# Attention and SwiGLU on one core: matrix products grouped by array shape, weights converted 1536 columns at a time with paced loads, gains on another queue

## The chip, the cores and the metric

The kernel runs on one core of a Trainium2 chip. The metric is the device time of one execution in microseconds (us), as the median of several runs. Engines are called TensorE (PE in the profile, PEld for its weight loads), VectorE (DVE), ScalarE (ACT), GpSimd (POOL) and SyncE (SP, which here only issues transfers).

## The reference, cut to what matters

```python
# q, k, v: (8, 12, 448, 64); d_model 768, d_ff 1536; the weights come as float64
q_n, k_n = rmsnorm(q, g_q), rmsnorm(k, g_k)
attn = softmax(q_n @ k_n.T / 8)
x = (attn @ v) -> (3584, 768)
g = x @ w_gate
out = (g * sigmoid(g) * (x @ w_val)) @ w_out
```

## The kernel before

Two heads are a "pair"; a batch has 6 pairs, and there are 48. The MLP works on 7 blocks of 512 tokens. Block n needs the attention of batches n and n+1. So batches 0 and 1 (12 "early" pairs) come first, together with the conversion of the float64 weights to float32, done by bit operations on ScalarE and VectorE. After that, the attention of batch n+2 is fitted in beside block n.

The program itself writes the order of the instructions. Every piece of work (one or some instructions of one engine) is registered with an estimated duration, a wished time `when`, and what it depends on. A small list scheduler at build time then simulates the engines and emits the pieces in the order that it finds:

```python
def start(self, piece):
    at = self.free.get(piece["engine"], 0.0)
    ...
    for before in piece["after"]:
        if before["end"] is None:
            return None
        at = max(at, before["end"] + 0.1)
    ...  # and the users of the buffers that it takes
# run(): for each engine, the first piece in order of `when`, unless another
# can start more than 0.02 us sooner
```

For one pair, scores `S_j = K_j^T Q` for four quarters j use 64 rows of the array for each head (row tiling). The weighted sums use 64 columns for each head (column tiling), with four quarters accumulated in PSUM (the memory that TensorE writes its sums to), and a fifth product with ones for the denominator. (Early pairs do the denominator in all four quarters.) The MLP and the transposes use the full array:

```python
when = base + (j // 2) * span * 0.4 + (j % 2) * 0.1          # score j
... 
last = add("PE", 1.55 if early else 0.8,                     # weighted sum j
           base + span * (0.55 + (j // 2) * 0.25) + (j % 2) * 0.1,
           lambda j=j: weighted(j), after=[ex[j], load_v, last], ...)
```

A part of the weights (768 columns) is loaded to a staging place inside tiles that are not in use yet, then takes six instructions:

```python
loaded = add("SP", 0.45, when - 14.0, lambda: nc.sync.dma_start(raw, src), after=[before], kb=768)
one   = add("ACT", 0.91, when, ... activation(dst, hi, AF.Abs) ...)
two   = add("ACT", 0.91, when, ... activation(lo, lo, AF.Copy, scale=2.0**-29) ...)
three = add("DVE", 0.56, when, ... tensor_scalar_max(dst, dst, LEAST) ...)
four  = add("DVE", 0.57, when, ... tensor_scalar(shift left 3, and) ...)
five  = add("DVE", 0.97, when, ... scalar_tensor_tensor(and, or) ...)
six   = add("DVE", 0.97, when, ... tensor_tensor(add) ...)
```

## Time and profile before

| | before |
|---|---|
| time, median | 1863.93 us (1863.9 to 1864.73) |
| first up projection of block 0 | 200.29 us |
| changes of array shape on TensorE before / after that point | 75 / 479 |
| from there to the end of the last matmul | 1657.8 us |
| TensorE, VectorE busy between 20 and 150 us | 110.2 / 107.4 of 130 us |
| mean granted TensorE clock between 20 and 150 us | 0.92 |

Read it as two programs one after the other. Up to 200 us, waits among all engines set the time; from then on TensorE is never idle for more than 0.6 us at a time. The lines are shown in the prediction. A change of array shape is counted where two neighbouring TensorE pieces use different tilings (full, 64 rows, 64 columns).

### The profile page before, as it was taken

What the parts mean: (1) busy time and instruction counts of PE and PEld (TensorE: products, weight loads), DVE (VectorE), ACT (ScalarE), POOL (GpSimd) and SP (SyncE); (2) the same over time, 40 slices, a digit from 0 to 9 for tenths busy, and PEclk for the clock granted to TensorE, in tenths of its full rate; (3) what the DMA queues carried; (4) which work ended last, traced back from release to release, by engine and by line L of the source; (5) the groups of instructions that cost most, each with busy time, mean ns of one, the idle gap of its engine ahead of it and who ended that gap; (6) DMA issues with size and microseconds to landing.
All of it is one profiled execution on the core that took longest, in us unless ns stands there. A gap on an engine that the chain in (4) does not pass through costs nothing.

```text
span 1863.5 us, 13867 instructions
## 1 busy us (share of the span) xinstructions
PE 1806.0 (97%) x5616; PEld 780.7 (42%) x5616; DVE 497.3 (27%) x568; ACT 387.6 (21%) x556; POOL 507.2 (27%) x264
## 2 busy tenths in 40 slices
PE   5788999999999999999999999999999999999998
PEld 2322344444444443444434444444444333444455
DVE  5887711132211231112231122221123121101100
ACT  6865310122101220102211022110122111100000
POOL 3784420254100542104432025320155122200000
PEclk9899999999999999999999999999999999999999
DMA  9645200011000110001110011100011000000000
GB/s 284 198 138 166 75 10 0 18 58 33 5 10 14 43 34 24 10 2 36 46 31 10 0 33 43 39 10 0 14 43 45 13 5 11 13 18 5 0 9 27
DMA packets 55053, 73.35 MB, mean 39 GB/s; under 512 B 4804, under 2 KB 44228, under 8 KB 54980
## 3 DMA queue, kind: packets, MB, share of 16 engines
q1 hardware_dynamic: 45888, 61.35, 11.1%
q10 hardware_dynamic: 8964, 11.02, 2.0%
q8 instruction: 46, 0.75, 0.2%
q14 instruction: 27, 0.22, 0.0%
q0 software_dynamic: 128, 0.00, 0.0%
HBM read 61.34 MB, written 11.01 MB: 39 GB/s over the span
## 4 chain that ended last, share of the span: by engine, by line
PE 92%; issue 3%; POOL 2%; ACT 1%; DVE 1%; ACTq 0%; POOLq 0%
PE mm L872 47%; PE mm L932 24%; PE at L705 11%; PE st L658 8%; PE st L620 2%; POOL rr L588 1%; POOL t L600 1%; ACT e L668 1%; DVE inv L744 0%; DVE QT L641 0%; ACT KT L633 0%; DVE wo L852 0%; DVE wo L845 0%; ACT wo L820 0%; ACT wo L824 0%
## 5 line engine op out<-in xcount | busy, mean ns | idle before, releaser
L932 PE MATMUL mm<-wo,gt 128*128 128x384 f32 x1344 | 458.4, 493 | 0.6 <-ACT rows L942 0.6
L872 PE MATMUL mm<-xT,wv 128*128 128x512 f32 x1008 | 450.7, 596 | 0.6 <-ACT rows L942 0.6
L872 PE MATMUL mm<-xT,wg 128*128 128x512 f32 x1008 | 450.3, 596 | 0.0
L932 PEld LDWEIGHTS mm<-wo,gt 128*128 128x128 f32 x1344 | 248.0, 190 | 218.4 <-issue 61.1
L872 PEld LDWEIGHTS mm<-xT,wv 128*128 128x128 f32 x1008 | 188.0, 190 | 249.8 <-issue 248.6
L674 POOL TENSOR_TENSOR sums<-e 112x896 f32<-112x896 f32 x36 | 75.2, 2089 | 790.2 <-ACT e L668 790.2
L872 PEld LDWEIGHTS mm<-xT,wg 128*128 128x128 f32 x1008 | 187.8, 190 | 244.1 <-issue 222.4
L668 ACT ACTIVATE e<-st 112x896 f32<-112x896 f32 x192 | 172.1, 916 | 333.2 <-PE st L658 251.3
L588 POOL TENSOR_TENSOR rr<-ss,minus_half 112x16 f32<-112x16 f32 x48 | 169.9, 3541 | 203.8 <-DVE ss L580 202.3
L744 DVE RECIPROCAL inv<-at 128x448 f32<-128x448 f32 x48 | 141.8, 2955 | 236.1 <-PE at L705 236.1
L658 PE MATMUL st<-QT,KT 64*112 64x448 f32 x768 | 190.7, 594 | 11.5 <-DVE QT L641 6.4
L882 ACT ACTIVATE gt<-mm 128x512 f32<-128x512 f32 x84 | 50.2, 597 | 689.4 <-PE mm L872 689.4
L705 PE MATMUL at<-e,v 112*64 112x448 f32 x768 | 188.7, 570 | 3.0 <-DVE inv L744 2.9
L677 POOL TENSOR_TENSOR sums<-sums,e 112x896 f32<-112x896 f32 x72 | 149.5, 2076 | 128.2 <-ACT e L668 126.1
L885 DVE SCALAR_TENSOR_TENSOR gt<-gt,mm 128x512 f32<-128x512 f32 x84 | 57.7, 687 | 435.9 <-ACT gt L882 435.9
L890 DVE SCALAR_TENSOR_TENSOR gt<-gt,mm 128x512 f32<-128x512 f32 x84 | 57.7, 687 | 338.9 <-PE mm L872 338.9
L658 PEld LDWEIGHTS st<-QT,KT 64*112 64x112 f32 x768 | 57.5, 177 | 136.2 <-issue 88.0
L600 POOL TENSOR_TENSOR t<-qk,rr 112x512 f32<-112x512 f32 x96 | 110.5, 1170 | 3.2
L641 DVE TENSOR_SCALAR QT<-st,gg 128x448 f32<-128x448 f32 x42 | 28.5, 678 | 254.9 <-ACT KT L633 254.5
L942 ACT COPY rows<-mm 128x384 f32<-128x384 f32 x56 | 26.8, 478 | 312.5 <-PE mm L932 312.5
L705 PEld LDWEIGHTS at<-e,v 112*64 112x64 f32 x768 | 39.7, 136 | 112.8 <-issue 102.0
L620 PE MATMUL st<-ident,t 112*128 112x112 f32 x384 | 50.0, 273 | 34.8 <-POOL t L600 31.9
(55 smaller groups left out, 525.2 us busy)
## 6 DMA issues: line engine op xcount, KB each, us to landing
qk<-in_q_dram SPq DMA_DIRECT2D x48, 224.0 KB, 2.8
qk<-in_k_dram SPq DMA_DIRECT2D x48, 224.0 KB, 2.9
v<-in_v_dram SPq DMA_DIRECT2D x48, 224.0 KB, 2.8
wo<-in_moe_w_out_dram SPq DMA_DIRECT2D x8, 768.0 KB, 4.3
gt<-in_moe_w_gate_dram SPq DMA_DIRECT2D x6, 768.0 KB, 12.0
gt<-in_moe_w_val_dram SPq DMA_DIRECT2D x6, 768.0 KB, 14.3
wo<-in_moe_w_gate_dram SPq DMA_DIRECT2D x6, 768.0 KB, 12.8
wo<-in_moe_w_val_dram SPq DMA_DIRECT2D x6, 768.0 KB, 11.5
```

The source lines that it names most:

```text
L588: nc.gpsimd.tensor_tensor(out=rr.rearrange("p x h j one -> p (x h j one)"), in0=tiles["ss", m], in1=minus_half, op=ALU.pow,)
L600: nc.gpsimd.tensor_tensor(out=tiles["t", m][:, :, x].rearrange("p j h d -> p h j d"), in0=tiles["qk", (m, x)], in1=tiles["rr", m][:, x].to ...
L620: nc.tensor.transpose(ps[:, x, ts(j, R)], tiles["t", m][:, j, x].rearrange("p h d -> p (h d)"), ident[0:R, 0:R],)
L658: nc.tensor.matmul(st[0:R, h, 0:S], tiles["KT", m][rows, j, :], tiles["QT", m][rows].rearrange("p j r -> p (j r)"), start=True, stop=True,)
L668: nc.scalar.activation(e, tiles["st", (m, j)][0:R, :, 0:S], AF.Exp)
L674: nc.gpsimd.tensor_tensor(out=to, in0=tiles["e", (m, 0)], in1=e, op=ALU.add)
L677: nc.gpsimd.tensor_tensor(out=to, in0=to, in1=e, op=ALU.add)
L705: nc.tensor.matmul(to[ds(D * h, D), 0:S], lhs(h), rhs[:, h], start=first, stop=last)
L744: nc.vector.reciprocal(inv, tiles[den][:, 0:S])
L872: nc.tensor.matmul(ps, w[:, f // 2, c, ts(f % 2, P)], xT[:, c, ts(n % 2, TB)], start=(c == 0), stop=(c == NW - 1),)
L885: nc.vector.scalar_tensor_tensor(gt[:, f], gt[:, f], 1.0, tiles["mm", (n, f, 0)], op0=ALU.add, op1=ALU.mult)
L932: nc.tensor.matmul(ps[:, 0:HALF], gt[:, f, ts(i, P)], wo[:, f, ts(half, HALF)], start=(f == 0), stop=(f == NF - 1),)
```

## The change

Its intent: change the array shape less often; give the first pairs of the attention priority over the conversion of the weights; and save instructions. Its core (cuts marked by `...`):

```diff
-            at = max(at, before["end"] + 0.1)
+            at = max(at, before["end"] + 0.1 * (before["engine"] != piece["engine"]))
...
+        if piece["early"] is not None:
+            at = max(at, piece["when"] - piece["early"])
...  # run(): a piece of the group just issued goes next if it can start within 0.7 us
+                    if last["group"] and piece["group"] == last["group"] and at < self.free[engine] + 0.7:
+                        choice = (at, piece)
+                        break
...  # scores: two and two, one right after the other
-            when = base + (j // 2) * span * 0.4 + (j % 2) * 0.1
+            when = base + (j // 2) * 0.4 + (j % 2) * 0.01
+                group=("s", m, j // 2), mode="rows",
...  # weighted sums and denominator: one group, after the first scores of the next pair
+        late = c == NPAIR - 1 and not early
+        when = base + span * 0.8 if late else sum(pair_time(m + 1)[:1]) + 0.2
+                after=(ex if j == 0 else []) + [load_v, last], group=("w", m), mode="columns",
...  # weights: 18 parts of 1536 columns
-        when = 8.0 + 5.0 * n
+        when = 12.0 + 11.0 * n
-            "SP", 0.45, when - 14.0, ..., after=[before], kb=768
+            "SP", 0.45, when - 16.0, ..., after=[staged.get(place)], kb=1536, early=2.0,
...  # queries of all early pairs on ScalarE (before: of every second one)
-            if early and m % 2:
+            if early:
...  # gains
-        nc.gpsimd.dma_start(t[0:64, :], col)
+        nc.scalar.dma_start(t[0:64, :], col)
-    nc.vector.scalar_tensor_tensor(out=gg, in0=gq2, scalar=8.0, in1=gk2, ...)
+    scaled_gains = order.add("DVE", 0.2, 9.0, lambda: nc.vector.scalar_tensor_tensor(out=gg, ...), early=0.0)
```

The loads of q, k and v also got `early=25.0`, and up projections wait in the model for the end of the block before.

More of the change, by code (lines that the diff above doesn't have):

```diff
@@ L361 @@
 class Order:
+    SWITCH = 0.17
     def __init__(self, pools):
@@ L378, in __init__, with add @@
         self.dma = 0.0
-    def add(self, engine, us, when, emit, after=(), takes=(), uses=(), port=False, kb=0):
+        self.last = {}
+    def add(
+        self, engine, us, when, emit, after=(), takes=(), uses=(), port=False, kb=0, group=None,
+        mode=None, early=None,
+    ):
         piece = dict(
             engine=engine, us=us, when=when, emit=emit, takes=takes, port=port, kb=kb,
+            group=group, mode=mode, early=early,
             after=[a for a in after if a is not None], end=None, n=len(self.pieces),
@@ L414, in run @@
                 choice = None
+                last = self.last.get(engine, dict(group=None))
                 for piece in pieces[:lookahead]:
                     at = self.start(piece)
-                    if at is not None and (choice is None or at < choice[0] - 0.02):
+                    if at is None:
+                        continue
+                    if (
+                        last["group"]
+                        and piece["group"] == last["group"]
+                        and at < self.free[engine] + 0.7
+                    ):
+                        choice = (at, piece)
+                        break
+                    if choice is None or at < choice[0] - 0.02:
                         choice = (at, piece)
@@ L427, in run @@
             end = at + piece["us"]
+            last = self.last.get(piece["engine"])
+            if piece["mode"] and last and last["mode"] != piece["mode"]:
+                end += self.SWITCH
+            self.last[piece["engine"]] = piece
             self.free[piece["engine"]] = end
@@ L513, in fast @@
     FIRST = LEAD + EARLY * PAIR + 10.0
-    UP, DOWN, BOTH = 122.0, 63.0, 113.0
+    UP, DOWN, BOTH = 123.6, 63.0, 113.0
     def block_start(n):
@@ L548, in load @@
             when = base - (26.0 if name == "qk" else 16.0)
-            return add("SP", 0.45, when, emit, takes=[(name, key)], kb=224)
+            return add("SP", 0.45, when, emit, takes=[(name, key)], kb=224, early=25.0)
         loaded = [load("qk", (m, x), src) for x, src in enumerate((q, k))]
@@ L626, in attention @@
         transposed = add(
-            "PE", 0.95, base - 3.0, transpose, after=scaled, uses=[("t", m)],
-            takes=[("st", (m, "t"))],
+            "PE", 0.8, base - 3.0, transpose, after=scaled, uses=[("t", m)],
+            takes=[("st", (m, "t"))], mode="full",
         )
@@ L647, in attention @@
         qt = add(
-            "ACT" if early and m % 2 else "DVE", 0.68, base - 1.5, queries, after=[transposed],
+            "ACT" if early else "DVE", 0.68, base - 1.5, queries, after=[transposed],
             takes=[("QT", m)], uses=[("st", (m, "t"))],
@@ L680, in attention @@
         for j in range(NJ):
-            when = base + (j // 2) * span * 0.4 + (j % 2) * 0.1
+            when = base + (j // 2) * 0.4 + (j % 2) * 0.01
             st = add(
-                "PE", 0.82, when, lambda j=j: scores(j), after=[kt, qt],
+                "PE", 0.75, when, lambda j=j: scores(j), after=[kt, qt],
                 uses=[("KT", m), ("QT", m)], takes=[("st", (m, j))],
+                group=("s", m, j // 2), mode="rows",
             )
@@ L723, in attention @@
             last = add(
-                "PE", 1.55 if early else 0.8,
-                base + span * (0.55 + (j // 2) * 0.25) + (j % 2) * 0.1,
-                lambda j=j: weighted(j), after=[ex[j], load_v, last],
+                "PE", 1.5 if early else 0.75, when + j * 0.01, lambda j=j: weighted(j),
+                after=(ex if j == 0 else []) + [load_v, last],
                 takes=([av, den] if early else [av]) if j == 0 else [],
                 uses=[("e", (m, j)), ("v", m)] + ([av] + [den] * early if j else []),
+                group=("w", m), mode="columns",
             )
@@ L737, in attention @@
             last = add(
-                "PE", 0.9, base + span * 0.95, total, after=[last, adds[-1]],
-                uses=[("sums", m)], takes=[den],
+                "PE", 0.75, when + 0.05, total, after=[last, adds[-1]],
+                uses=[("sums", m)], takes=[den], group=("w", m), mode="columns",
             )
@@ L746, in attention @@
         inv = add(
-            "DVE", 2.96, base + span, invert, after=[last], uses=[den], takes=[("inv", m)]
+            "DVE", 2.96, when + 4.0, invert, after=[last], uses=[den], takes=[("inv", m)]
         )
@@ L766, in attention @@
         done_x[m] = add(
-            "DVE", 0.66, base + span + 1.0, divide, after=[inv] + [up_done[n] for n in blocks],
+            "DVE", 0.66, when + 5.0, divide, after=[inv] + [up_done[n] for n in blocks],
             uses=[av, ("inv", m)],
@@ L781, in weight_parts, with weight_part @@
         gate, val = (w.rearrange("(c p) f -> p c f", p=P) for w in (moe_w_gate, moe_w_val))
+        places = [("gt", 0), ("gt", 1), ("wo", 0), ("wo", 1), ("wo", 2)]
         n = 0
         for f in range(NF // 2):
-            for half in range(2):
-                for w, dst, name in ((gate, wg, "g"), (val, wv, "v")):
-                    cs = ts(half, NW // 2)
-                    where = n % 10
-                    stage = ("gt", where) if where < 4 else ("wo", where - 4)
-                    yield w[:, cs, ts(f, 2 * P)], dst[:, f, cs, :], (NW // 2, 2 * P), (name, f), stage
-                    n += 1
+            for w, dst, name in ((gate, wg, "g"), (val, wv, "v")):
+                yield w[:, :, ts(f, 2 * P)], dst[:, f], (NW, 2 * P), (name, f), places[n % 5]
+                n += 1
         rows = moe_w_out.rearrange("(f p) c -> p f c", p=P)
-        for f in range(NF):
-            stage = ("wo", (5, 4, 3)[f % 3]) if f < 8 else ("gt", 2 + f % 2)
-            yield rows[:, f : f + 1, :], wo[:, f : f + 1, :], (1, DM), ("o", f), stage
+        for f, place in enumerate((4, 3, 4, 4, 1, 1)):
+            fs = ts(f, 2)
+            yield rows[:, fs, :], wo[:, fs, :], (2, DM), ("o", f), places[place]
     weights = {}
     staged = {}
-    def weight_part(n, src, dst, shape, what, stage):
-        a, b = shape
-        before = staged.get(stage)
-        when = 8.0 + 5.0 * n
-        region, s = stage
+    def weight_part(n, src, dst, shape, what, place):
+        when = 12.0 + 11.0 * n
+        region, s = place
         if region == "gt":
-            raw = gt[:, ts(s, NF // 4), :].rearrange("p f t -> p (f t)")
+            raw = gt[:, ts(s, NF // 2), :].rearrange("p f t -> p (f t)")
         else:
-            raw = wo[:, ts(s, 2), :].rearrange("p f c -> p (f c)")
-        raw = raw.bitcast(I64).rearrange("p (a b) -> p a b", a=a)
+            raw = wo[:, ts(s, NF // 3), :].rearrange("p f c -> p (f c)")
+        raw = raw.bitcast(I64).rearrange("p (a b) -> p a b", a=shape[0])
         words = raw.bitcast(U32).rearrange("p a (b two) -> p a b two", two=2)
@@ L815, in weight_part @@
         loaded = add(
-            "SP", 0.45, when - 14.0, lambda: nc.sync.dma_start(raw, src), after=[before], kb=768
+            "SP", 0.45, when - 16.0, lambda: nc.sync.dma_start(raw, src),
+            after=[staged.get(place)], kb=1536, early=2.0,
         )
@@ L819, in weight_part @@
         one = add(
-            "ACT", 0.91, when, lambda: nc.scalar.activation(dst, hi.bitcast(F32), AF.Abs),
+            "ACT", 1.55, when, lambda: nc.scalar.activation(dst, hi.bitcast(F32), AF.Abs),
             after=[loaded, *clear],
@@ L823, in weight_part @@
         two = add(
-            "ACT", 0.91, when, lambda: nc.scalar.activation(lo, lo, AF.Copy, scale=2.0**-29),
+            "ACT", 1.55, when, lambda: nc.scalar.activation(lo, lo, AF.Copy, scale=2.0**-29),
             after=[loaded],
@@ L827, in weight_part @@
         three = add(
-            "DVE", 0.56, when, lambda: nc.vector.tensor_scalar_max(dst, dst, LEAST),
+            "DVE", 0.95, when, lambda: nc.vector.tensor_scalar_max(dst, dst, LEAST),
             after=[one], port=True,
@@ L831, in weight_part @@
         four = add(
-            "DVE", 0.57, when,
+            "DVE", 0.97, when,
             lambda: nc.vector.tensor_scalar(
@@ L843, in weight_part @@
         five = add(
-            "DVE", 0.97, when,
+            "DVE", 1.77, when,
             lambda: nc.vector.scalar_tensor_tensor(
@@ L850, in weight_part @@
         six = add(
-            "DVE", 0.97, when,
+            "DVE", 1.77, when,
             lambda: nc.vector.tensor_tensor(out=bits, in0=bits, in1=lo, op=ALU.add),
@@ L854, in weight_part @@
         )
-        staged[stage] = six
-        weights.setdefault(what, []).append(six)
+        staged[place] = weights[what] = six
     down_done = {}
@@ L894, in block @@
         hidden = []
-        last = None
+        last = down_done.get(n - 1)
         for f in range(NF):
@@ L900, in block @@
                     add(
-                        "PE", 5.05, start + (2 * f + which) * step,
+                        "PE", 5.15, start + (2 * f + which) * step,
                         lambda f=f, which=which: gate_value(f, which),
                         after=[done_x[m] for m in tokens]
-                        + (weights["gv"[which], f // 2] if n == 0 else []) + [last],
-                        takes=[("mm", (n, f, which))],
+                        + ([weights["gv"[which], f // 2]] if n == 0 else []) + [last],
+                        takes=[("mm", (n, f, which))], mode="full",
                     )
@@ L909, in block @@
             when = start + 2 * f * step + 1.0
-            before = [down_done[n - 1]] if n else [staged.get(("gt", f // 3))]
+            before = [down_done[n - 1]] if n else [staged.get(("gt", f // (NF // 2)))]
             t = add(
@@ L964, in block @@
                     + (
-                        [w for f in range(part * NF // 2, (part + 1) * NF // 2) for w in weights["o", f]]
+                        [weights["o", f // 2] for f in range(part * NF // 2, (part + 1) * NF // 2)]
                         if n == 0 else []
                     ),
-                    takes=[key] * (1 - part), uses=[key] * part,
+                    takes=[key] * (1 - part), uses=[key] * part, mode="full",
                 )
@@ L986, in fast @@
         col = x.rearrange("(d one) -> d one", one=1)
-        nc.gpsimd.dma_start(t[0:64, :], col)
-        nc.gpsimd.dma_start(t[64:128, :], col)
+        nc.scalar.dma_start(t[0:64, :], col)
+        nc.scalar.dma_start(t[64:128, :], col)
     make_identity(nc, ident)
     nc.gpsimd.memset(ones, 1.0)
-    nc.vector.scalar_tensor_tensor(
-        out=gg, in0=gq2, scalar=8.0, in1=gk2, op0=ALU.mult, op1=ALU.mult
+    scaled_gains = order.add(
+        "DVE", 0.2, 9.0,
+        lambda: nc.vector.scalar_tensor_tensor(
+            out=gg, in0=gq2, scalar=8.0, in1=gk2, op0=ALU.mult, op1=ALU.mult
+        ),
+        early=0.0,
     )
```

## The prediction

> **What bounds the kernel now.** I read the page's slices first, then the chain of waits, then the timeline of TensorE.
>
> ```profile
> PE 1806.0 (97%) x5616; PEld 780.7 (42%) x5616; DVE 497.3 (27%) x568; ACT 387.6 (21%) x556; POOL 507.2 (27%) x264
> ...
> PE   5788999999999999999999999999999999999998
> ...
> DVE  5887711132211231112231122221123121101100
> PEclk9899999999999999999999999999999999999999
> ...
> PE 92%; issue 3%; POOL 2%; ACT 1%; DVE 1%; ACTq 0%; POOLq 0%
> ```
>
> A slice is 46.6 us. The first four or five hold the attention of two batches and the conversion of the weights (12 early pairs of heads); there TensorE has holes and VectorE is at 7 to 8 tenths. From then on TensorE is full, so every microsecond of TensorE work saved there is saved in the end. The windows of the early stretch (columns: length, busy of PE, PEld, DVE, ACT, POOL, clock, DMA share, GB/s):
>
> ```profile
> 0.00:10.00 10.00, 0.00 (x0) 0.00 (x0) 0.56 (x3) 2.74 (x4) 3.19 (x12) 1.00 0.58 168
> 10.00:20.00 10.00, 0.00 (x0) 0.00 (x0) 6.08 (x10) 4.61 (x6) 4.67 (x2) 1.00 1.08 285
> ...
> 40.00:60.00 20.00, 13.00 (x58) 5.33 (x56) 18.65 (x24) 15.08 (x21) 8.31 (x4) 0.75 0.92 267
> 60.00:80.00 20.00, 17.17 (x74) 5.90 (x72) 16.05 (x21) 17.39 (x23) 17.48 (x6) 0.82 0.63 192
> ```
>
> TensorE does nothing for 20 us, then loses 7 us of the 20 after 40 us, while the queues move 267 to 380 GB/s of weights. The first cause is on VectorE and GpSimd:
>
> ```profile
> 13.66 0.16 DVE L991 SCALAR_TENSOR_TENSOR gg<-gq,gk 128x1 f32<-128x1 f32 x1 [9.53 <-DMA gk<-in_g_k_dram]
> 13.74 1.21 DVE L579 TENSOR_REDUCE ss<-t 112x16 f32<-112x1024 f32 x1
> ...
> 20.84 2.01 PE L620 MATMUL st<-ident,t 112*128 112x112 f32 x8 [20.84 <-POOL t L600]
> ```
>
> ScalarE had squared the first q and k by 5.56 us, but VectorE stood behind the product of the two gains, whose DMA landed only at 13.6. Now a stretch of the full phase; the third view shows what a change of array shape costs:
>
> ```profile
> 262.62 5.42 PE L872 MATMUL mm<-xT,wg 128*128 128x512 f32 x12
> 267.97 1.01 PE L658 MATMUL st<-QT,KT 64*112 64x448 f32 x4
> 268.91 5.42 PE L872 MATMUL mm<-xT,wv 128*128 128x512 f32 x12
> 274.17 5.31 PE L872 MATMUL mm<-xT,wg 128*128 128x512 f32 x12
> 279.31 5.31 PE L872 MATMUL mm<-xT,wv 128*128 128x512 f32 x12
> ...
> 339.93 0.97 PE L705 MATMUL at<-e,v 112*64 112x448 f32 x4
> 340.83 4.14 PE L932 MATMUL mm<-wo,gt 128*128 128x384 f32 x12
> 344.90 0.97 PE L705 MATMUL at<-e,v 112*64 112x448 f32 x4
> ```
>
> From start to start (the durations overlap), twelve up-projection instructions take 5.15 us when the next has the same shape (274.17 to 279.31) and 5.35 before a score (262.62 to 267.97). A score takes 0.94 before a full-array matmul, but 0.75 when another score follows (eight in 1.69). A weighted sum takes 0.90 before a down projection and 0.75 before another weighted sum. So each change costs 0.15 to 0.20 us.
>
> **What the Trainium skill says.** (1) "TensorEngine Tiling (Array Packing)", section "Key Properties": "Changing tiling mode (not just tile) drains the TensorE". The trace agrees: the 0.15 to 0.20 us above appear at changes between 64-row, 64-column and full, while two tiles of one mode already run side by side (four 448-column instructions in 0.75 us, where 12 of 512 columns in 5.15 us give 0.43 for one). (2) "ScalarE: Activation LUTs", section "What ACT_TABLE_LOAD costs", gives an activation with immediates 186 ns plus 0.833 ns a column. The trace has copies of 384 columns at 478 ns and 448 at 532: slope 0.84, fixed part about 155 ns. Wider instructions save only that part. (3) "GPSIMD Engine Reference", section "Specifications": its SBUF interfaces are shared with VectorE, with contention when VectorE runs two-port or two-input instructions. The trace fits it: the inverse root on GpSimd takes 2.9 us in quiet stretches, 10.3 at 58 us, 9.0 at 119.9. (4) "DMA: Bandwidth & Descriptors", section "Specifications", first byte about 1 us by GpSimd's queue, 0.6 by ScalarE's. The trace has 6.8 and 9.1 us to landing for the gains by GpSimd's queue, so the wait is more than that difference; part must be the traffic of 768 KB loads it lies among.
>
> **The change part by part.**
>
> *Grouping, after block 0 begins.* Up projections start at 200.29 us. From there the timeline has 478 changes of shape; the start-to-start surplus over the same-shape times, kind by kind, sums to about 84 us (for example 74 down-to-weighted at 0.20, 68 weighted-to-down at 0.15, 40 up-to-weighted at 0.20, 37 up-to-score at 0.20, 39 score-to-up at 0.19). After it: the four weighted sums and the denominator of a pair go as one group of five (3.75 us), placed just after the first two scores of the next pair, and its other two scores just after it. In the best order that is full, rows, columns, rows, full: 4 changes. ScalarE has the time for it: the first weighted sum frees its e buffer after 0.75 us, and two exponentials of 0.92 end about 2.7 us into the group, so the next two scores can start at its end. A batch then has 4 for its first pair's scores alone, 5 x 4, and 2 for the last group: 26. Where the scores are not ready right behind the transpose (keys and queries take 1.2 to 1.3 us, the idle before scores in the early timeline), the weighted group runs first and there are 5 instead; I add 3 per batch. 6 x 29 = 174 changes at 0.175 = 30 us. Saved: 84 - 30 = 54 us, all on the path.
>
> *Block borders.* Block n+1 can't start before the last pair's reciprocal (2.96) and multiply (0.6). The last pair's group is placed 15 us after its scores, ahead of about three down-projection parts (3 x 3.87 = 11.6 us), so that lies hidden. Before, about 1.0 us of idle stood at each of five borders (0.44, 0.33, 0.27); I expect at most that.
>
> *The head.* The gains go by ScalarE's queue and are no longer first on VectorE. First sum of squares at about 5.7 instead of 13.74; inverse root 3.0, two scalings 2.3, transpose at about 12.7 instead of 20.84; keys and queries 1.3; first score about 14.9 instead of 24.19: 9.3 us earlier. The four gain DMAs are issued on ScalarE, about 0.3 us each before the squares; counted in.
>
> *Wider conversions.* VectorE, single-source: 0.55 at 768 columns, fixed part about 0.15 (from the multiplies of 128 columns at 287 ns and 448 at 619), so 0.95 at 1536; two-source 0.95 becomes 1.75. Start to start, instructions of 768 follow at 0.47 and 0.87, so two halves cost 5.36 and one whole part 5.08 by the same overlap. For 18 parts that is only 5 us of VectorE; ScalarE saves 36 x 0.15 = 5 us as well. All queries of even early pairs move to ScalarE: 6 x 0.6 = 3.6 us off VectorE.
>
> *Pacing.* A load of 1.57 MB may start no sooner than every 11 us (143 GB/s) instead of at once. With q, k and v of a pair (0.69 MB) the queues need some 200 GB/s, where 380 was reached, so pairs 2 and 3 should no longer wait (their transposes came at 52.6 and 69.5, after 16 to 17 us each). It also pushes the conversion of w_out behind: by the time block 0 starts, VectorE must have done 12 pairs x 4.75 (sums 1.3, reciprocal 2.9, multiply 0.55) = 57, 12 gate and value parts x 5.08 = 61 and about 3 of w_out = 15: 133 us, where it was busy for 157 us before 200. At the same density as before (157 of 186 us from 13.7 on) from 5.7 on: 5.7 + 133/0.84 = 164 us.
>
> *The early pairs on TensorE.* Ideal: 0.8 + 4 x 0.75 + 4 x 1.5 + four changes = 10.5 us. The longest cycle: the weighted group of pair m+1 needs the two PSUM buffers of pair m, that is its reciprocal and multiply, 4 us after that group's end. Meanwhile TensorE has the two scores (1.5), waits for an exponential to free a score buffer (about 0.4), transposes (0.8), waits for keys and queries (1.3), and does two scores (1.5): 5.5 us, which hides the 4. With the group (6.0) and the changes: 12.2 us a pair, where pairs 3 to 11 took 125 us, 13.9 each. The first score at 14.9 plus 11 x 12.2 = 149, then the last pair: 1.5 + 0.5 + 6.2 + 1.5 for its scores, some 2 for exponentials and PSUM, 6.2 for its group, 4 for reciprocal and multiply = 22: 171 us. VectorE's sum gives 164, the longer counts: 172 for the start of block 0, 28 us before the 200.3 now. Part of the work of later pairs that filled holes there (22 scores instructions and 16 of transposes, 5.5 us) is held back by the pacing of q and k and comes in the full phase.
>
> *Sum of the full phase.* Up 168 x 5.16 = 866.9; down 112 x 3.87 = 433.4; 36 pairs x (0.8 + 3.0 + 3.75) = 271.8; changes 30; idle 5; copy and store at the end and unexplained rest 6 (the same sum for before, with its 84, gives 1657 against the 1663 measured): 1613. 172 + 1613 = 1785 us, 4.2% less.
>
> **The rivals.** *The early phase keeps its bound.* If VectorE and GpSimd contend as now, pairs stay at 13 to 13.9 us and only the head is won: block 0 at 36 + 11 x 13.5 = 185, total about 1798. For it: VectorE at 85%, inverse roots of 7.6 and 9.0 us in the chain; wider two-source instructions hold the shared interface longer at a time. Against: the stalls at 46.7 and 67 follow loads in a full queue. *A wait replaces the changes of shape.* Five weighted products in a row bunch the evacuation: if scores wait for the e ring of four, or the group for GpSimd's running sum (three times 2.1 us), TensorE idles, or each pair costs 6 changes. Six give 36 x 6 + 12 = 228, 40 us: total 1795; with 1 us idle per pair as well, 1831. Against: there is nearly always a ready projection to run. *Borders stall.* If the last group came after all down projections, 4 us more at each of 5 borders: 1805. *The better way:* the early pairs reach the ideal 10.5: block 0 at about 155, total 1768.
>
> **Range and chances.** 1785 us; 8 in 10 between 1762 and 1808: the early phase is uncertain by about 15 us each way, the count of changes by 8, idle by 5. Two per cent faster is under 1826.6; to miss it both parts must fail by half. Faster 0.96, within 2% 0.035, slower 0.005.
>
> **What would show it.** First transpose near 13 us and first score near 15; up projections from about 172; weighted groups of 20 instructions in about 3.9 us with scores beside them; about 174 changes of shape in the full phase instead of 478; borders with no idle of over 1.5 us; VectorE's instructions on weights halved in number, 0.95 and 1.75 us each. It would be wrong if TensorE showed holes in the full phase, if the first up projection came after 190, or if the changes of shape stayed above 250.

## The result, and the profile after

The changed kernel took 1767.05 us (median of 4 runs, 1764.52 to 1768.01) beside 1864.33 for the kernel before: ratio 0.9476, 95% interval 0.9459 to 0.9492. A ratio here is the mean time of one kernel's fast runs over that of the other's of the same rounds, so it is not quite the ratio of the medians. The forecast was 1785 with a range of 1762 to 1808.

The busy totals and slices of the changed kernel:

```profile
PE 1733.2 (98%) x5616; PEld 807.7 (46%) x5616; DVE 482.6 (27%) x490; ACT 381.3 (22%) x526; POOL 487.6 (28%) x260
...
PE   5999999999999999999999999999999999999998
...
DVE  6997512221223111122111222122321222111100
...
PEclk9999999999999999999999999999999999999999
```

The same 5616 matmul instructions cost TensorE 73 us less busy time. It is full from the second slice on (now 44 us each), and the clock has no dip in the first slices. The windows that answer to those before (same columns as in the prediction) show TensorE at 94 and 95% and VectorE at 98%:

```profile
40.00:60.00 20.00, 18.80 (x98) 6.90 (x94) 19.69 (x15) 14.27 (x18) 13.71 (x7) 1.00 0.71 229
60.00:80.00 20.00, 18.95 (x104) 7.80 (x104) 19.59 (x16) 14.98 (x19) 12.03 (x7) 1.00 0.54 173
```

A stretch of the full phase, from TensorE's timeline (start, duration, what):

```profile
291.46 1.76 PE L682 MATMUL st<-QT,KT 64*112 64x448 f32 x8
293.16 3.23 PE L730 MATMUL at<-e,v 112*64 112x448 f32 x16
296.21 0.92 PE L730 MATMUL at<-sums,ones 112*64 112x448 f32 x4
297.07 1.76 PE L682 MATMUL st<-QT,KT 64*112 64x448 f32 x8
298.76 8.01 PE L955 MATMUL mm<-wo,gt 128*128 128x384 f32 x24
```

This is the order that the prediction calls best: two scores, five weighted products (293.16 to 297.07, 3.91 us from start to start, against 5 x 0.75 = 3.75 without a change), two scores, and two parts of a down projection with no change between them. And one cycle of an early pair:

```profile
105.69 0.96 PE L644 MATMUL st<-ident,t 112*128 112x112 f32 x8 [0.36 <-ACT e L692]
106.58 0.97 PE L730 MATMUL at<-e,v 112*64 112x448 f32 x4
...
112.74 1.76 PE L682 MATMUL st<-QT,KT 64*112 64x448 f32 x8
114.83 1.82 PE L682 MATMUL st<-QT,KT 64*112 64x448 f32 x8 [0.33 <-ACT e L692]
117.01 0.96 PE L644 MATMUL st<-ident,t 112*128 112x112 f32 x8 [0.36 <-ACT e L692]
```

The transpose comes every 11.32 us (105.69 to 117.01). The weighted group of the pair before stands between a pair's transpose and its scores. So the keys and queries are copied while TensorE works, and the only idle left is 0.33 and 0.36 us, where an exponential has to free a score buffer.

In numbers: the first up projection came at 156.69 us instead of 200.29 (43.6 sooner), and from there to the end of the trace it is 1608.6 us instead of 1663.2 (54.6 shorter). Together that is 98.2 us, the difference of the two traces. After that point there are 168 changes of shape; the surplus over same-shape starts sums to 31 us, against 85 by the same sum before. (The sum: each stretch of one shape, from its start to the start of the next and without idle time, less its instructions at the pace that they keep among their like: 0.429 us for an up instruction, 0.323 for a down one, 0.188 for a score or weighted sum, 0.099 for a transpose.)

The 43.6 us of the early phase are not waits alone. TensorE's idle time before the first up projection fell from 45.8 to 25.3 us, 20.4 less. Its busy time there fell from 154.5 to 131.3 us. Of these 23 us, about 5 are transposes and scores of later pairs (16 and 20 instructions) that now come in the full phase, and about 7 are the 40 changes of shape less (75 to 35, at 0.18 each). The rest, some 11 us by this estimate, goes with the granted clock, whose mean up to that point was 0.93 before and is 1.00 now; what moves the clock no run here isolates.

The head (the first 25 us) of the kernel, from the timeline of all engines:

```profile
5.43 1.22 DVE L603 TENSOR_REDUCE ss<-t 112x16 f32<-112x1024 f32 x1 [1.69 <-ACT t L585]
11.04 2.01 PE L644 MATMUL st<-ident,t 112*128 112x112 f32 x8 [11.04 <-POOL t L624]
13.38 0.16 DVE L1016 SCALAR_TENSOR_TENSOR gg<-gq,gk 128x1 f32<-128x1 f32 x1 [6.52 <-DMA gk<-in_g_k_dram]
13.68 1.58 ACT L844 ACTIVATE wg<-gt 128x1536 f32<-128x1536 f32 x1 [8.28 <-DMA gt<-in_moe_w_gate_dram]
...
17.69 0.54 ACT L657 COPY KT<-st 128x448 f32<-128x448 f32 x1
18.10 0.66 ACT L663 ACTIVATE QT<-st,gg 128x448 f32<-128x448 f32 x1
18.82 6.14 PE L682 MATMUL st<-QT,KT 64*112 64x448 f32 x16 [5.77 <-ACT QT L663]
```

The first sums and the first transpose are 8 and 10 us earlier than before. The first score is only 5.4 us earlier (18.82 instead of 24.19): ScalarE had been given a conversion ahead of the keys and waited for its load until 13.68. And the gains landed at 13.4 by ScalarE's queue, as they did at 13.7 by GpSimd's.

### The profile page after: what moved, and what is told of

It reads as the page before. It is cut to its first block, busy times and chain, and to the rows that moved or that the text cites. A ratio compares the mean times of both kernels' runs of the same rounds, so it can differ in the third digit from the quotient of the medians.

```text
span 1765.2 us, 13688 instructions
## 1 busy us (share of the span) xinstructions
PE 1733.2 (98%) x5616; PEld 807.7 (46%) x5616; DVE 482.6 (27%) x490; ACT 381.3 (22%) x526; POOL 487.6 (28%) x260
## 4 chain that ended last, share of the span: by engine, by line
PE 93%; POOL 3%; issue 2%; ACT 1%; DVE 1%; POOLq 0%; ACTq 0%; DVEq 0%
PE mm L895 49%; PE mm L955 25%; PE at L730 10%; PE st L682 7%; POOL rr L612 2%; PE st L644 2%; POOL t L624 1%; ACT e L692 1%; DVE inv L773 0%; DVE wo L869 0%; DVE wo L876 0%; ACT wo L844 0%; DVE wo L852 0%; DVE wo L857 0%; DVE xT L783 0%
## 5 line engine op out<-in xcount | busy, mean ns | idle before, releaser
L955 PE MATMUL mm<-wo,gt 128*128 128x384 f32 x1344 | 447.9, 490 | 0.0
L612 POOL TENSOR_TENSOR rr<-ss,minus_half 112x16 f32<-112x16 f32 x48 | 149.1, 3107 | 800.4 <-DVE ss L604 739.8
L692 ACT ACTIVATE e<-st 112x896 f32<-112x896 f32 x192 | 165.6, 914 | 240.8 <-PE st L682 165.3
L682 PE MATMUL st<-QT,KT 64*112 64x448 f32 x768 | 172.3, 568 | 10.5 <-ACT QT L663 6.9
L730 PE MATMUL at<-e,v 112*64 112x448 f32 x768 | 161.1, 546 | 0.2 <-DVE inv L773 0.2
L730 PEld LDWEIGHTS at<-e,v 112*64 112x64 f32 x768 | 50.9, 136 | 87.2 <-issue 80.7
L665 DVE TENSOR_SCALAR QT<-st,gg 128x448 f32<-128x448 f32 x36 | 24.6, 684 | 193.1 <-ACT KT L657 193.1
L603 DVE TENSOR_REDUCE ss<-t 112x16 f32<-112x1024 f32 x48 | 58.4, 1217 | 14.7 <-ACT t L585 14.7
```

What stands on the lines that cost most here:

```text
L603: nc.vector.tensor_reduce(out=ss, in_=sq, axis=AX.X, op=ALU.add)
L612: nc.gpsimd.tensor_tensor(out=rr.rearrange("p x h j one -> p (x h j one)"), in0=tiles["ss", m], in1=minus_half, op=ALU.pow,)
L682: nc.tensor.matmul(st[0:R, h, 0:S], tiles["KT", m][rows, j, :], tiles["QT", m][rows].rearrange("p j r -> p (j r)"), start=True, stop=True,)
L692: nc.scalar.activation(e, tiles["st", (m, j)][0:R, :, 0:S], AF.Exp)
L730: nc.tensor.matmul(to[ds(D * h, D), 0:S], lhs(h), rhs[:, h], start=first, stop=last)
L955: nc.tensor.matmul(ps[:, 0:HALF], gt[:, f, ts(i, P)], wo[:, f, ts(half, HALF)], start=(f == 0), stop=(f == NF - 1),)
```

## The experiments

Theory: in the full phase each change of array shape costs TensorE 0.15 to 0.20 us, and their number is all that matters. In the early phase the pacing and the order of the head free the attention of waits. Rivals: the full phase got shorter through something else; the early phase got shorter because VectorE's instructions are wider, or through the new queue. The table gives all runs. "Full" is from the first up projection to the end of the last matmul; the changes are counted in the program's order. No run undoes the queries on ScalarE, the hold on q, k and v, or the model's new estimates of durations by themselves.

| run | time, us | ratio to before | first up projection | changes after it | full, us |
|---|---|---|---|---|---|
| before | 1864.3 | 1 | 200.3 | 479 | 1657.8 |
| changed | 1767.05 | 0.9476 | 156.7 | 168 | 1603.0 |
| group_alone | 1816.63 | 0.9745 | 203.2 | 164 | 1605.9 |
| gap_alone | 1816.33 | 0.9743 | 176.8 | 307 | 1632.1 |
| group_undone | 1803.7 | 0.9676 | 160.7 | 307 | 1636.1 |
| group_gap_undone | 1858.6 | 0.9973 | 177.0 | 500 | 1673.1 |
| weights_undone | 1798.7 | 0.9643 | 182.9 | 168 | 1609.0 |
| weights_narrow | 1772.51 | 0.9504 | 157.5 | 168 | 1607.4 |
| loads_unpaced | 1794.33 | 0.9620 | 185.7 | 168 | 1601.3 |
| conversions_paced | 1786.25 | 0.9576 | 170.5 | 168 | 1608.7 |
| gains_first | 1770.77 | 0.9495 | 160.4 | 168 | 1602.9 |
| gains_pool | 1769.21 | 0.9484 | 161.6 | 168 | 1602.9 |
| best | 1775.05 | 0.9519 | 159.4 | 168 | 1607.7 |
| changed_again | 1767.35 | 0.9478 | 156.4 | 168 | 1602.8 |

All results were correct. The 95% intervals of the ratios are 0.0017 wide to each side or less, but for group_gap_undone (0.0020).

### The number of changes of shape

**group_alone**: the kernel before with the scheduler, groups, modes and placements of the changed one; weights, gains, queries and the hold on q, k and v as before.

```diff
-  (before) scores spread over the pair, weighted sums one by one, 0.1 us between dependent pieces
+  (changed) group=("s", m, j // 2), group=("w", m), mode=..., 0.1 * (before["engine"] != piece["engine"])
```

> The kernel before with the grouping alone (groups, modes and the scheduler's model of them; conversions of 768 columns unpaced, gains by GpSimd's queue and first on VectorE, queries as before). Changes of array shape after the first up projection: 164 instead of 479, in the early phase 33 instead of 75. If each change costs TensorE some 0.175 us and nothing else fills it: full phase 55 us shorter, early phase up to 7 us shorter, 1800 to 1812 us in all. If the full phase got shorter for another reason (weights, loads): within 10 us of 1864.

1816.6 us, 4.6 above the range. The full phase is 52 us shorter, as expected, but the early phase got no shorter at all (203.2).

**group_gap_undone**: the opposite. In the changed kernel the placement and the model are as before.

```diff
-        at = max(at, before["end"] + 0.1 * (before["engine"] != piece["engine"]))
+        at = max(at, before["end"] + 0.1)
-            when = base + (j // 2) * 0.4 + (j % 2) * 0.01
+            when = base + (j // 2) * span * 0.4 + (j % 2) * 0.1
-  weighted sums: group=("w", m), after the next pair's first scores
+  weighted sums: one by one, as before, no group
```

> The changed kernel with the grouping undone: weighted sums and scores placed as before, no groups, and the 0.1 us that the scheduler's model put between two dependent instructions of one engine put back; weights, pacing, gains and queries stay changed. 500 changes of shape in the full phase, 75 in the early phase. Cost-per-change theory: 332 x 0.17 = 56 us longer there and up to 7 us early, 1820 to 1832 us. Rival, that the order of work and the pacing carry the gain: under 1785.

1858.6 us: 27 above the range, and only 5.5 below the kernel before. The full phase is 70 us longer than with groups. Of that some 9 are idle (10.4 us instead of 1.2), so (1673.1 - 10.4 - 1601.9) / 332 = 0.18 us for each change. The early phase lost another 20 us, which the count (75 instead of 35 changes) does not pay for.

**gap_alone**: the kernel before with one line.

```diff
-            at = max(at, before["end"] + 0.1)
+            at = max(at, before["end"] + 0.1 * (before["engine"] != piece["engine"]))
```

> The kernel before with one line changed: the scheduler's model puts no 0.1 us between two dependent instructions of the same engine. 307 changes of shape in the full phase instead of 479, 49 early instead of 75. Cost per change 0.17: 29 us less in the full phase, 4 early: 1830 us. If cost depends on grouping in fours and fives and not on the count: nearer 1864.

1816.3 us, almost half of the whole gain by one constant of a model. It shows where 172 of the 479 changes came from. By the code, a weighted sum depends on the one before it, on the same engine. The model let it start 0.1 us later than a projection that was ready, so the projection went between them, though on the chip such neighbours follow with no gap (0.75 us from start to start). The full phase fell by 26 us for 172 changes, near the 29 expected. The early phase fell by 23.5, where I had expected 4. About 5 us of that are no gain: they are the later pairs' transposes and scores (16 and 20 instructions), which stood in the early phase of the kernel before and are in the full phase here. For the rest see the last part of this section.

**group_undone**: the changed kernel without groups and placements, but with the corrected model.

```diff
-                group=("s", m, j // 2), mode="rows",
+                mode="rows",
-                group=("w", m), mode="columns",
+                mode="columns",
   (and both `when` as before)
```

> The changed kernel with groups and placements undone, but the corrected 0.1 us kept: 307 changes in the full phase, 43 early. Cost per change: 139 x 0.17 = 24 us more, early 1 to 3 more: 1790 to 1794. A point on the line between 168 and 500 changes; off the line if something else than the count matters.

1803.7 us, 10 above the range. 8.7 us are idle, 7.5 more than with groups. Without them the 139 additional changes cost (1636.1 - 8.7 - 1601.9) / 139 = 0.18 us each; gap_alone gives 0.17 by the same sum. Four programs with 168, 307, 307 and 500 changes thus lie near one line, 0.17 to 0.18 us for each: the count is what matters, and the full phase of the theory stands. The kernel before lies on it too once the 5 us of work that it did early are added (0.18). The clock is no rival here: it was granted at 1.00 in the full phase of all of them but for short dips in block 0 (0.83 for 10 us in group_undone, 0.86 for 12 in group_gap_undone), worth 2 us each. What I missed is that a less tidy order also waits a little more.

### The weights

**weights_undone**: 36 parts of 768 columns, unpaced, and the old staging places, in the otherwise changed kernel.

```diff
-  18 parts, kb=1536, early=2.0, when = 12.0 + 11.0 * n
+  36 parts, kb=768, when = 8.0 + 5.0 * n
```

> The changed kernel with the whole handling of the weights as before (36 parts of 768 columns, loads not held back, old staging places); grouping, gains and queries stay changed. The grouping alone left the first up projection at 203 us. If the handling of the weights is what grouping needs: first up projection at 190 to 203 us, 1800 to 1815 us in all. If the head (gains) and the queries on ScalarE carry the early gain: first up projection at 158 to 168, 1768 to 1780.

1798.7 us, a little under the first range: the first up projection is 26 us later (182.9), and block 0 then waits 5.4 us for the last early pair (1.2 in the changed kernel). The handling of the weights carries 32 us of the whole. Beside group_alone (203.2) it also shows that gains, queries and the hold on q and k are worth 20 us when the weights are not paced.

**weights_narrow**: width alone.

```diff
-            "ACT", 1.55, when, lambda: nc.scalar.activation(dst, hi.bitcast(F32), AF.Abs),
+            "ACT", 1.82, when, twice(lambda a: nc.scalar.activation(dst[:, a], hi[:, a].bitcast(F32), AF.Abs)),
   (the same for all six; `a` runs over two halves)
```

> The changed kernel with each conversion instruction of 1536 columns split in two of 768 in the same place; loads, pacing and all else unchanged. From the prediction's sums the width saves 5 us of VectorE and 5 of ScalarE over 18 parts: first up projection 2 to 6 us later, 1769 to 1773 us. If VectorE is the bound of the early phase its whole busy difference shows (some 8 us or more, 1775); if the width does not matter, 1767.

1772.5 us, in the range: the width is worth 5 us. But the sum behind the range is wrong, so that hit is luck. On VectorE one part takes 5.35 us in halves, from the start of the first to that of what follows (154.74 to 160.09), and 5.56 whole (153.18 to 158.74): each wide instruction depends on the one before and starts after its end, while the halves of two parts of the same step overlap. So no time was saved along such a chain. The first up projection is only 0.8 us later; 0.5 us more idle follows before its last product, and 2.2 us before a later up projection of block 0 that waits for VectorE.

**loads_unpaced**: the hold on the weight loads taken out.

```diff
-            after=[staged.get(place)], kb=1536, early=2.0,
+            after=[staged.get(place)], kb=1536,
```

> The changed kernel without the hold on the weight loads (q, k and v keep theirs). If pacing carries the early gain, because queues full of weights delay q and k as before: first up projection 10 to 30 us later, 1777 to 1797. If the two staging places and their release already pace the loads: within 4 us of 1767.

1794.3 us: this one argument is worth 27 us, all of it before block 0. Windows and TensorE's timeline of this run:

```profile
20.00:40.00 20.00, 15.31 (x68) 5.89 (x66) 17.08 (x13) 18.45 (x18) 9.45 (x3) 0.90 1.06 366
40.00:60.00 20.00, 15.23 (x62) 5.58 (x58) 19.66 (x15) 15.14 (x15) 8.57 (x3) 0.76 0.98 327
```

```profile
30.55 0.98 PE L644 MATMUL st<-ident,t 112*128 112x112 f32 x8
35.16 2.50 PE L682 MATMUL st<-QT,KT 64*112 64x448 f32 x8 [3.62 <-ACT QT L663]
38.50 3.33 PE L682 MATMUL st<-QT,KT 64*112 64x448 f32 x8 [0.84 <-ACT e L692]
...
50.22 0.60 PE L644 MATMUL st<-ident,t 112*128 112x112 f32 x4 [1.70 <-POOL t L624]
52.73 0.70 PE L644 MATMUL st<-ident,t 112*128 112x112 f32 x4 [1.91 <-POOL t L624]
```

The queues move 327 to 366 GB/s again, and the clock falls to 0.76. After the transpose at 31 us the scores wait 3.6 us for the queries, and at 50 the transposes wait for the scaled q and k. The hold is one of the build-time model; on the chip nothing waits for a clock time. What it changes is the place of the weight loads in SyncE's order: in the changed kernel the second to sixth are issued at 14.0, 15.6, 30.4, 38.2 and 51.6 us, here at 14.0, 15.0, 15.5, 17.1 and 26.1. Here the third pair's q is therefore issued at 20.3 us, behind five of them, and in the changed kernel at 14.6, behind two. From 108 us on, this run has the same cycle of 11.32 us as the changed kernel; it lost its time on the pairs before that and never gets it back.

**conversions_paced**: is it the queue, or conversions that push ahead of the attention on ScalarE and VectorE? Here the loads run free and the first two conversion instructions are held.

```diff
-            after=[staged.get(place)], kb=1536, early=2.0,
+            after=[staged.get(place)], kb=1536,
-            after=[loaded, *clear],
+            after=[loaded, *clear], early=0.0,
-            after=[loaded],
+            after=[loaded], early=0.0,
```

> The changed kernel with the hold moved from the weight loads to the first two conversion instructions on ScalarE: the loads are issued as soon as a staging place is free, the conversions keep their pace of one part per 11 us. Without any hold the first up projection came at 185.7 us (1794). If the full queues alone delay q and k, it stays at 178 to 190, 1786 to 1798 us. If the harm is that conversions run ahead of the attention's work on ScalarE and VectorE, it comes back to 157 to 163, 1767 to 1774 us.

1786.3 us, at the edge of the first range; the first up projection, at 170.5, lies between the two that were expected. Both are part of it. With the wait before the last product of the first up projection (5.6 us here, 1.2 in the changed kernel) counted in, the start is at 176.2, against 157.9 with loads paced and 185.7 with nothing paced: 18 us belong to the loads, 9.5 to the conversions. In the first 60 us q and k took 10.5 and 7.8 us to land (medians), in the changed kernel 2.7 and 5.7; first the lines of this run, then those of the changed kernel:

```profile
qk<-in_q_dram SPq DMA_DIRECT2D x6, 224.0 KB, 10.5
qk<-in_k_dram SPq DMA_DIRECT2D x6, 224.0 KB, 7.8
...
qk<-in_q_dram SPq DMA_DIRECT2D x7, 224.0 KB, 2.7
qk<-in_k_dram SPq DMA_DIRECT2D x7, 224.0 KB, 5.7
```

That the split is exact is not shown, since both runs have another order of work too.

### The head and the gains

**gains_first**: the product of the gains first on VectorE again.

```diff
-    scaled_gains = order.add("DVE", 0.2, 9.0, lambda: nc.vector.scalar_tensor_tensor(out=gg, ...), early=0.0)
+    nc.vector.scalar_tensor_tensor(out=gg, ...)
```

> The changed kernel with the product of the gains again first on VectorE, ahead of the first sums of squares (its DMA still on ScalarE's queue). The first transpose should fall back from 11 to about 20 us, as that DMA landed at 13.3. But the first score stood at 18.8 behind ScalarE's conversions, so the cost in the end is smaller: first up projection 2 to 5 us later, 1769 to 1772. If the whole 9 us of the head pass on: 1776.

1770.8 us, in the range. The first transpose came at 20.06 and the first score at 23.23, 4.4 us after the changed kernel's; 3.7 us of it arrive at the end.

**gains_pool**: the gains by GpSimd's queue, nothing else.

```diff
-        nc.scalar.dma_start(t[0:64, :], col)
+        nc.gpsimd.dma_start(t[0:64, :], col)
   (all four)
```

> The changed kernel with the gains loaded by GpSimd's queue again, their product still behind the first sums of squares on VectorE. The gains landed at 13.4 us by ScalarE's queue and at 13.7 by GpSimd's before, so the queue should not matter: within 2 us of 1767, first transpose at 11 to 13.5 us (GpSimd issues four transfers first, 2.3 us). If the queue carried the head's gain: 1772 or more.

1769.2 us (1768.1 to 1771.8): 2 us slower by the medians, and the intervals of the two ratios overlap (0.9469 to 0.9500 against 0.9464 to 0.9492), so a loss is not shown. The first transpose was no later (10.6), the first score 2 us later. The profiled run is the slowest of the four (1771.8); its first up projection came 5 us later. So the queue carries some 2 us at the most in the median; the place in VectorE's order carries 3.7 (gains_first).

**best**: an attempt to repair the head. Weight loads start 14 us later, so that the keys of the first pair stand ahead of the first conversion on ScalarE.

```diff
-        when = 12.0 + 11.0 * n
+        when = 12.0 + 11.0 * n + (max(0.0, 32.0 - 2.0 * n) if n > 11 else 0.0)
-            kb=1536, early=2.0,
+            kb=1536, early=-12.0,
```

> An attempt to beat the changed kernel: weight loads may start 14 us later than in it (so the first keys and queries stand ahead of the first conversion on ScalarE, and the gains and the second q and k are not in its traffic), and the first four parts of w_out start 8, 6, 4 and 2 us later still, so that the last early reciprocal is not behind them on VectorE. First score at 14 to 15 us instead of 18.8, first up projection at 150 to 153 instead of 157: 1760 to 1764 us. If the pairs after the first are held by VectorE and not by the head: 1766 to 1768.

**changed_again**: the changed kernel beside it.

> The changed kernel unaltered, beside the attempt on the same chip, for a comparison of a few tenths of a per cent: 1764 to 1768 us.

1775.05 us against 1767.35: the attempt lost, and neither of its two forecasts was right. Its timeline, three engines:

```profile
14.74 5.36 PE L682 MATMUL st<-QT,KT 64*112 64x448 f32 x16 [1.16 <-ACT QT L663]
...
159.53 2.96 DVE L773 RECIPROCAL inv<-at 128x448 f32<-128x448 f32 x1 [5.78 <-PE at L730]
...
167.91 0.62 DVE L783 TENSOR_TENSOR xT<-at,inv 128x448 f32<-128x448 f32 x1
...
168.58 2.07 PE L895 MATMUL mm<-xT,wg 128*128 128x512 f32 x2 [4.60 <-DVE xT L783]
```

The head did what it should: the first score came at 14.74. But by the fifth pair the lead was gone: its transpose waited 1.3 us for the scaled q and k from GpSimd and came at 60.38 (60.42 in the changed kernel), and the sixth at 74.48 (71.74). At the end VectorE was given a whole part of w_out between the last early reciprocal and its multiply, 162.4 to 167.9, while TensorE stood for 4.6 us. The reason can be read in the code: the wished time of these two pieces is taken from the next pair, and the next pair of the last early one is planned some 100 us later, so any conversion goes ahead of them. The changed kernel has the same weakness, with a reciprocal that is ready at 156.9 and starts at 158.74; a version with only that mended was not run.

### What stays open

The early phase does not add up. With the old weights it ends at 200.3 (old order), 176.8 (corrected model) and 203.2 (groups); with the new weights at 177.0, 160.7 and 156.7. So groups help only together with the new weights, and with the old ones they undo what the corrected model alone brings. In group_alone TensorE is idle for 36 us between its first transpose and the first up projection (22 in gap_alone), and its clock between 20 and 150 us is 0.87 (0.96). By the traces, 13.3 of the 36 us are scores that wait for queries and 10.3 transposes that wait for GpSimd (8.5 and 6.2 in gap_alone), but no run takes apart which wait starts it.

## Why the prediction was right

**Changes of shape.** 174 changes were forecast, 168 measured; 30 us of surplus against 31. The 54 us of that step came out as 54 by the same sum (85 less 31). Two further terms nearly cancel: idle time fell by 5 us, and the 5.5 us of later work that used to fill early holes came back, as foreseen. The trace agrees with what the page "TensorEngine Tiling (Array Packing)", section "Key Properties", says of a drain at a change of mode; 168 to 500 changes at 0.17 to 0.18 us show its size here.

**Borders.** At most 1 us each was forecast; at block borders the trace shows no idle of 0.15 us or more. The one wait is before the last product of the first up projection of block 0 (1.16 us).

**The head.** This step failed. "First score about 14.9: 9.3 us earlier" became 18.82, 5.4 us earlier. The transposes were early (11.0 against 12.7), but ScalarE works in its order and a conversion stood in front of the keys; its load, 1.5 MB, landed 12 us after it was issued. The prediction counted the four issues on ScalarE and not what the scheduler would place there. It also gave the new queue a share that it does not have (gains_pool).

**The pair.** "12.2 us a pair" was 11.32. The term that was wrong is the 1.3 us of waiting for keys and queries: the weighted group of the pair before fills it. I had put the group after the first two scores. That the order is transpose, weighted group, four scores I put down to the four e buffers (they hold the exponentials of the scores), which the weighted group has to free before the next exponentials; that is read in the code, and no run tests it.

**Start of block 0.** 172 was forecast and 156.7 measured (157.9 with the wait behind it). Three errors add up to the 15 us: the first score was 4 us later than forecast, eleven pairs at 0.9 us less are 10 us earlier, and the tail after the last pair took some 9 us less than the 22 that I added for its scores, group and reciprocal. In the trace the last weighted group ends at 156.7, and five of the six products of the first up projection run beside the reciprocal.

**Width and pacing.** The width was given 5 us of VectorE and 5 of ScalarE. The kernel lost 5 us without it, but not in that way: a whole part takes 5.56 us on VectorE where 5.08 was forecast, no less than in halves. The pacing was right as a mechanism (the loads hold up q and k of pairs 2 and 3), and is the larger part of the early gain: 27 us.

**Rivals.** "The early phase keeps its bound" fell, though VectorE is now busy for 98% there: in the cycle above TensorE waits only for exponentials, 0.7 us a pair. VectorE has next to no room left, so whether pairs could come faster than 11.3 us is not shown. "A wait replaces the changes" and "borders stall" fell too. "The better way" (1768) is the time that came, but not by its mechanism: the pairs stayed at 11.3 instead of the ideal 10.5, and the overlap at the end made up for it. That its number fits to 1 us is luck. The forecast was 18 us too high, of which 15 are the early phase; that is the whole margin that it gave that phase.

**What it did not see.** The line with the 0.1 us was in the diff and the prediction passed over it. Alone it accounts for 172 of the 479 changes of shape before, and for 48 us.

## What to carry to other kernels

When TensorE is full, count its changes of array shape in the trace and compare start to start with the same instruction next to its like; an order that puts like beside like is bought with no arithmetic. Where a build-time model orders the work, read what it believes of a gap as closely as the kernel: a tenth of a microsecond between dependent instructions of one engine made 172 changes. And don't load early what is needed late: the same bytes, placed later in the order of the loads by a hold in the model, made the whole 27 us shorter, while a fix of the head that looked safe lost 8 us further on.

## What the Trainium skill lacked or had wrong

- "TensorEngine Tiling (Array Packing)", section "Key Properties": names the drain at a change of mode and gives no size. Here, for float32 products of 384 to 512 columns, single pieces cost 0.20 us from full to 64 rows or 64 columns, 0.19 from rows and 0.15 from columns back; after a whole group of columns it is 0.16. The mean over 168 to 500 changes is 0.17 to 0.18 us.
- "DMA: Bandwidth & Descriptors", section "Specifications": gives the first-byte latencies of the two kinds of queue (about 0.6 and 1 us) and no time to landing for a tiny transfer beside large ones. Here the gains (0.2 KB) took 7.1 and 10.0 us to land by ScalarE's queue and 6.8 and 9.1 by GpSimd's.
- No page that I read says what a wide instruction on VectorE costs, from start to start, when it depends on the one before: here a chain of four takes 5.56 us at 1536 columns and 5.35 us as eight of 768 in pairs, so halving the number of instructions saved nothing there.
